# Squares of the gate's rows go between SBUF's quadrants in sixteen SyncE transfers for each half, where they were stored to DRAM and loaded again by ScalarE's queue

## The chip, the cores and the metric

The kernel runs on one core of a Trainium2 chip. The metric is the time of one execution on the device, in microseconds (us), as the median of several runs. Beside the runs there is one profiled execution with its own time; its trace is what the views below are taken from. Engines are called as the profile calls them: PE (TensorE matmul), DVE (VectorE), ACT (ScalarE), POOL (GpSimd), SP (SyncE, which only issues DMA transfers here); SPq and ACTq are the issuing instructions of SP and ACT.

## The reference

One transformer block on a sequence of 2048 rows of 512: softmax attention with 32 heads of 16, then a gated MLP whose gate mixes over the sequence. The change lies in the last stage, so the second half is what has to be seen (`S` = 2048, `D` = 512, `Fh` = 688):

```python
def _B_ref(x, w_in, w_sp, b_sp, w_out):
    z = _gelu(jnp.einsum("bsd,df->bsf", x, w_in))
    z1 = z[..., :Fh]
    z2 = _layernorm(z[..., Fh:], axis=-1)
    g = jnp.einsum("ts,bsf->btf", w_sp, z2) + b_sp[None, :, None]
    return jnp.einsum("bsf,fd->bsd", z1 * g, w_out)

h = x + _A_ref(_layernorm(x, axis=-1), A_wqkv, A_wo)
h2 = h + _B_ref(_layernorm(h, axis=-1), B_w_in, B_w_sp, B_b_sp, B_w_out)
```

## The kernel before

All operands of a matmul are split into a high and a low half-precision part, and a product is made of three matmuls (high by high, high by low, low by high; `mm3`, L108 to L110). Attention and the first projections take the program up to about 1290 us of the span, the making of `z` and of `h` up to about 1455 us, and the last stage, from L1471 on, the rest. Only that last stage is touched.

**The loop.** The gate's 2048 by 2048 product is done by Strassen's scheme in the form that needs seven products for two by two blocks. The loop at L1481 goes over eight pairs of row blocks, `p` = 0 to 7; pair `p` is rows `128 p` and `128 (p + 8)`. In each pass PE runs seven products by name, `b11`, `t1`, `t2`, `b22`, `t3`, `b21`, `n4`, each of 24 matmuls of 128x344 (`product`, L1304). ACT and DVE add the parts (`p1` L1492, `q5` L1496, `v` L1502, the sums at L1509, L1520, L1533, L1543), and POOL multiplies by `z1` (L1510, L1521, L1534). The result is the tile `pr`, 128 rows by two blocks by 688 columns, the gated rows z1 * g.

**The output projection, one pass late.** The gated rows of pair `p` must be turned (rows to columns) before PE can multiply them by `w_out`. They are handled in two halves of the columns: half 1 holds columns 384 to 687, half 0 columns 0 to 383. For each half `level` finds a power of two by which `raise_` (ACT, L1363) scales the rows, and `squares` (L1372) turns them on DVE, which turns 32x32 squares within each group of 32 partitions. What is left is to move whole squares between the four groups of 32 partitions (the quadrants). The tile `squares0` or `squares1` is read by partition group j and square column q, and the tile `whole0` or `whole1` must have at partition group q and place j what stood at partition group j and place q. Each such piece is 32 partitions by 192 numbers of 4 bytes (768 bytes in each partition, 24 KB).

**How it moves before.** `send` (L1385) stores the whole tile (384 KB) to a DRAM scratch `t_scr` with one transfer in ACT's queue; `bring` (L1389) loads it back in four transfers of 96 KB, one for each quadrant of the target, also in ACT's queue, and is called one pass later: `bring(1)` behind `p1`, `bring(0)` behind `q5`. Then `hi` (ACT, L1400) makes the high part of a half, `lo` (DVE, L1409 to L1415) the low part, and `multiply` (L1439) the products with `w_out` on PE. In the pass of pair `p`, `multiply(1, ...)` of pair `p - 1` (16 matmuls of 128x512) stands between the products `b22` and `t3`, and `multiply(0, ...)` (18 matmuls) between `t3` and `b21`. `gather` (DVE, L1454) adds them to the rows of `h`, and `store` (SP, L1457) writes these out.

**What sets the order.** `manual_schedule` (L1471) keeps the program's order on each engine. An engine takes its instructions one after another, so an instruction that waits holds back all that stand behind it on the same engine, DMA issues included. `product` ends with `ask` (L1158), which issues SP's load of a left operand (512 KB) for a product eight places further on; nine such tiles (`op`) exist. `fetch` (L1461) loads the two blocks of `z1` and of `h` for the pair after the current one at the start of each pass. All these are in SP's queue.

**Semaphores of transfers.** Each transfer is counted on one of eight semaphores, taken in turn by the transfers of SP and ACT in program order, and its issue waits until the transfer that last had the same semaphore has landed. So at most eight are on their way.

Of the kernel before, what the change touches and what calls it, by code (L numbers as in the profile page):

```python
# [8 lines left out]
F32 = mybir.dt.float32  # L9
# [10 lines left out]
P = 128  # L20
# [20 lines left out]
HF = 3 * P  # L41
# [18 lines left out]
def block_kernel(ctx: ExitStack, tc: tile.TileContext, x, wqkv, wo, w_in, w_sp4, b_sp, w_out, out):  # L60
# [7 lines left out]
    nc = tc.nc  # L68
# [3 lines left out]
    dram = ctx.enter_context(tc.tile_pool(name="dram", bufs=1, space=DRAM))  # L72
# [15 lines left out]
    h_scr = dram.tile([S, D], F32, name="h_scr")  # L88
    z_scr = dram.tile([S, FH], F32, name="z_scr")
    top_scr = dram.tile([1, 4 * P], F32, name="top_scr")  # L90
    t_scr = [dram.tile([P, 2 * HF], F32, name=f"t{i}_scr") for i in range(4)]
    m_scr = [dram.tile([P, 32], F16, name=f"m{i}_scr") for i in range(2)]
    op_scr = [{n: dram.tile([P, 2, HB, P], F16, name=f"{n}_{p}_scr") for n in TAKEN}
              for p in range(HB)]
# [175 lines left out]
    with ExitStack() as pre:  # L270
# [341 lines left out]
        for g in range(3):  # L612
            a, b = 4 * g, 4 * g + 4
# [54 lines left out]
        for j in range(24):  # L668
            b, n, i = 1 + j // 8, j // 2 % 4, 1 - j % 2
# [117 lines left out]
    with ExitStack() as at:  # L787
# [13 lines left out]
        def product(s, hg, qb, kb, p, t):  # L801

            r = slice(RG * t, RG * t + KM)
            nc.tensor.matmul(s, kst[hg % 2][r, p, kb * P:(kb + 1) * P],  # L804
                             qst[hg * NQ + qb][r, p, :], start=True, stop=True)
# [122 lines left out]
        def send():  # L928
            for i, key in enumerate(measured):
                nc.sync.dma_start(top_scr.rearrange("o (p i) -> (o p) i", i=4)[:, i:i + 1],  # L930
                                  sizes_of[key][:, :1])
# [88 lines left out]
        for key in measured:  # L1020
            for n in (256, 128, 64, 32, 16, 8, 4, 2, 1):
                halve(sizes_of[key], n, 1)
        soon(len(chores) + 4, send)
        soon(len(chores) + 9, spread)
        chores.extend([idle] * 18)
# [18 lines left out]
        for n in range(0, len(units), 2):  # L1044
# [53 lines left out]
            for tok in PAIR if len(later) < 2 else ():  # L1098
                i = int(tok[-1]) if tok[-1].isdigit() else 0
# [16 lines left out]
                elif tok == "H":  # L1116
                    a = 0 if first else 256
# [168 lines left out]
    with ExitStack() as fin:  # L1286
# [3 lines left out]
        f2 = fin.enter_context(tc.tile_pool(name="fin_2", bufs=2))  # L1290
# [5 lines left out]
        def next_g():  # L1296
            banks[0] += 1
            return ps_g[(banks[0] - 1) // 2 % 2].tile([P, 512], F32, name="g")[:, :FC]
# [21 lines left out]
        def weigh_w():  # L1320

            for i in range(2 * 3):
                nc.vector.tensor_reduce(w_top[:, i:i + 1], raw_w[:, i, :], axis=AX.X, op=ALU.max,
                                        apply_absolute_value=True)
# [14 lines left out]
        class Rows:  # L1339
# [43 lines left out]
                    nc.vector.transpose(t.rearrange("p q w i a -> p (w i) q a"), self.pr[:, :, :HF])  # L1383

            def send(self, half):  # L1385
                nc.scalar.dma_start(t_scr[2 * (self.p % 2) + half],
                                  self.turned[half].rearrange("p q w i a -> p (q w i a)"))

            def bring(self, half):  # L1389

                t = self.turned[half] = f2.tile([P, 4, 2, 3, 32], F32, name=f"whole{half}", bufs=1)
                src = t_scr[2 * (self.p % 2) + half].rearrange("(j b) (q c) -> q b j c", j=4, q=4)
                for q in range(4):
                    nc.scalar.dma_start(t[32 * q:32 * q + 32].rearrange("b j w i a -> b j (w i a)"), src[q])

            def hi(self, half):

# [63 lines left out]
        def fetch(p):  # L1461

            got = []
            for name, src, n in (("z1", z_scr, FH), ("h", h_scr, D)):
                for i in range(2):
                    t = fz.tile([P, n], F32, name=f"{name}{i}", bufs=2 + (name == "h"))
                    nc.sync.dma_start(t, src[rows(p, i), :])
                    got.append(t)
            return got

        with tc.manual_schedule(engines={E.PE, E.Activation, E.DVE, E.Pool, E.SP}):  # L1471
            wu = [f1.tile([P, 2 * 3, D], F16, name=f"wu{i}") for i in range(2)]
            raw_w = f1.tile([P, 2 * 3, D], F32, name="raw_w")
            w_top, w_low, w_up, w_down = [f1.tile([P, n], F32, name=f"w_{i}") for i, n in enumerate((6, 1, 1, 1))]
            nc.gpsimd.memset(raw_w[:, 2 * 3 - 1, :], 0.0)
            nc.sync.dma_start(raw_w[:, :5, :], w_out[:5 * P, :].rearrange("(i p) c -> p i c", p=P))
            for r0 in (TW - fn, P - fn):
                nc.sync.dma_start(raw_w[r0:r0 + fn, 5, :], w_out[5 * P:, :])
            nxt = fetch(0)
            now = None  # L1480
            for p in range(HB):  # L1481
                (z1t, z1b, ht, hb), last = nxt, p + 1 == HB
                nxt = None if last else fetch(p + 1)
                before, now = now, Rows(p, (ht, hb))
                bt, bb = bias_up[:, p:p + 1], bias_up[:, p + HB:p + HB + 1]
                A, C, B = [next_g() for _ in range(3)]
                p1, v, q5 = [f0.tile([P, FC], F32, name=n) for n in ("p1", "v", "q5")]
                left, right = now.pr[:, 0, :FC], now.pr[:, 0, FC:FH]
                bl, br = now.pr[:, 1, :FC], now.pr[:, 1, FC:FH]

                product(A, "b11")
                nc.scalar.activation(p1, A, AF.Identity, bias=bt)  # L1492
                if p:
                    before.bring(1)
                product(C, "t1")
                nc.scalar.activation(q5, C, AF.Identity, bias=bb)  # L1496
                if p:
                    before.bring(0)
                else:
                    weigh_w()  # L1500
                product(A, "t2", False)
                nc.scalar.activation(v, A, AF.Identity, bias=bt)  # L1502
                if p:
                    before.hi(1)
                    before.lo(1)
                    before.lower(1, 0, 1)
                    before.lower(0, 0, 1)
                product(C, "b22", False)
                nc.vector.tensor_add(right, C, v)  # L1509
                nc.gpsimd.tensor_mul(right, right, z1t[:, FC:])  # L1510
                if p:
                    accs = [before.multiply(1, w) for w in range(2)]
                    for w in range(2):
                        before.gather(1, w, accs[w])
                    before.hi(0)
                    before.lo(0)
                else:
                    measure_w()
                product(A, "t3", False)
                nc.vector.tensor_add(br, A, q5)  # L1520
                (nc.vector if last else nc.gpsimd).tensor_mul(br, br, z1b[:, FC:])  # L1521
                now.level(1, 0, 1)
                now.raise_(1, 0, 1)
                if p:
                    accs = [before.multiply(0, w) for w in range(2)]
                    for w in range(2):
                        before.gather(0, w, accs[w])
                        before.store(w)
                if not last:
                    now.squares(1)  # L1530
                    now.send(1)
                product(B, "b21")
                nc.vector.tensor_add(left, B, p1)  # L1533
                (nc.vector if last else nc.gpsimd).tensor_mul(left, left, z1t[:, :FC])  # L1534
                if last:
                    now.level(0, 0)
                    for w in range(2):
                        now.turn(1, w)
                        now.split(1, w)
                    now.lower(1, 0, 1)  # L1540
                    now.raise_(0, 0)
                product(A, "n4", False)
                nc.vector.scalar_tensor_tensor(bl, A, bb, z1b[:, :FC], op0=ALU.add, op1=ALU.mult)  # L1543
                if last:
                    now.level(0, 1)
                    now.raise_(0, 1)
                else:
                    now.level(0, 0, 1)
                    now.raise_(0, 0, 1)
                    now.squares(0)  # L1550
                    now.send(0)
            accs = [now.multiply(1, 0)]
            now.turn(0, 0)
            now.split(0, 0)
            accs.append(now.multiply(1, 1))
            now.turn(0, 1)
            now.gather(1, 0, accs[0])
            now.split(0, 1)
            now.gather(1, 1, accs[1])
            now.lower(0, 0, 1)  # L1560
            acc = now.multiply(0, 0)
            now.gather(0, 0, acc)
            now.store(0)
            acc = now.multiply(0, 1)
            for c in (slice(0, D // 2), slice(D // 2, D)):
                now.gather(0, 1, acc, c)
                now.store(1, c)
# [29 lines left out]
```

## Time and profile before

| | |
|---|---|
| Median of 3 runs | 1727.85 us (1726.92 to 1728.79) |
| The profiled execution | 1733.43 us, of which the span of the trace is 1731.7 us |
| Mean granted TensorE clock in it | 0.997 |
| PE busy from 0 to 1420 us | 1410.34 us |
| PE busy from 1420 to 1732 us | 295.05 us of 312.00 |
| DVE, ACT, POOL busy from 1420 to 1732 us | 135.38, 66.73, 51.70 us |
| DMA share and rate from 1420 to 1732 us | 0.57, 181 GB/s |

How to read the views that follow. A row of waits has the waiting engine and line, what it waited for, the total, the number of times and the longest. A row of the timeline has start, duration, engine, line, operation, output <- inputs, and in brackets the idle time of the engine just before it and what ended that. A row of windows has the stretch, its length, the busy time of PE, PEld, DVE, ACT and POOL with their instruction counts, the granted TensorE clock as a share of full speed, the busy share of the DMA engines, and their GB/s. A row for a line has the number of instructions after the x and least, median and greatest duration in ns.

### The profile page before, as it was taken

To read this page: it belongs to the slowest core of one execution; us is meant where nothing else is said; L and a number is where in the kernel's file an instruction comes from. 1 tells how busy PE (TensorE), PEld (TensorE's weight loads), DVE (VectorE), ACT (ScalarE), POOL (GpSimd) and SP (SyncE) were. 2 spreads that over 40 slices of the span, in tenths; PEclk is the share of its full clock that TensorE was granted. 3 is DMA by queue.
4 is the path that set the end of the run, shared out by engine and by line. 5 is a ranking of instruction groups with operands and counts; after the bars stand their busy time and mean duration, and the time that the engine had idled before them with its cause. 6 is when DMAs were issued, how large, how long until landed. Compare 5 with 4: busy or idle time off the path is not lost.

```text
span 1731.7 us, 36651 instructions
## 1 busy us (share of the span) xinstructions
PE 1705.4 (98%) x13499; PEld 644.6 (37%) x13499; DVE 1449.7 (84%) x3051; ACT 1318.0 (76%) x2584; POOL 812.9 (47%) x1062
## 2 busy tenths in 40 slices
PE   9999999999999999999999999999999999999999
PEld 4433222222222222222222222222226666565555
DVE  7688999999999999999999999999927886432434
ACT  4334999999999999999999999999984554111111
POOL 1332867775772268686677857300004676100100
PEclk9999999999999999999999999999999999999999
DMA  5534332342231235355245343310124455676661
GB/s 182 162 97 146 98 88 82 95 102 68 75 71 30 62 100 135 99 151 149 80 142 144 120 124 106 75 23 9 45 64 136 142 180 198 217 229 204 181 196 53
DMA packets 194013, 201.53 MB, mean 116 GB/s; under 512 B 66824, under 2 KB 142920, under 8 KB 193832
## 3 DMA queue, kind: packets, MB, share of 16 engines
q1 hardware_dynamic: 181448, 182.53, 36.4%
q10 hardware_dynamic: 12384, 16.65, 2.9%
q8 instruction: 106, 1.74, 0.4%
q14 instruction: 75, 0.61, 0.1%
HBM read 127.61 MB, written 71.44 MB: 115 GB/s over the span
## 4 chain that ended last, share of the span: by engine, by line
PE 71%; DVE 15%; DMA 6%; POOL 2%; issue 2%; ACT 2%; SPq 1%; ACTq 1%; DVEq 0%; POOLq 0%
PE pv L829 25%; PE s L804 17%; PE m L224 9%; DVE mx L229 7%; PE acc L108 4%; PE acc L110 4%; PE acc L109 4%; DMA whole<-t_scr 2%; PE g L110 2%; PE g L108 2%; PE g L109 2%; DVE ab L238 1%; DVE og L839 1%; DMA rc<-r_scr 1%; DVE rs_t L125 1%
## 5 line engine op out<-in xcount | busy, mean ns | idle before, releaser
L813 ACT ACTIVATE pt<-s 128x512 f32<-128x512 f32 x1968 | 1006.2, 637 | 5.5 <-PE m L224 4.4
L229 DVE TENSOR_REDUCE mx<-m 128x1 f32<-128x512 f32 x1510 | 947.5, 682 | 12.7 <-PE m L224 3.9
L804 PE MATMUL s<-qst,kst 50*128 50x512 f16 x2048 | 604.3, 379 | 0.2
L829 PE MATMUL pv<-pt,vst 128*32 128x256 f32 (+1 forms) x6056 | 598.1, 466 | 4.1 <-DVE og L839 1.3
L224 PE MATMUL m<-kst,qst 48*128 48x512 f16 x1510 | 452.5, 381 | 0.0
L804 PEld LDWEIGHTS <-kst 50*128 50x128 f16 x2048 | 132.0, 94 | 352.0 <-issue 322.9
L829 PEld LDWEIGHTS pv<-pt,vst 128*32 128x32 f32 x6056 | 119.5, 108 | 290.7 <-issue 277.3
L224 PEld LDWEIGHTS <-qst 48*128 48x128 f16 x2048 | 159.2, 93 | 173.7 <-issue 124.3
L224 PE MATMUL m<-uvs,qst 48*128 48x512 f16 x504 | 190.5, 380 | 0.6 <-DVE mx L229 0.6
L246 POOL TENSOR_SCALAR nm<-nm 128x16 f32<-128x16 f32 x32 | 6.6, 206 | 361.2 <-DVE nm L243 361.2
L238 DVE CUSTOM_DVE_ANT_0 ab<-m,ab 128x512 f32<-128x512 f32 x252 | 170.5, 677 | 2.7 <-ACT ab L234 2.7
L234 ACT ACTIVATE ab<-m 128x512 f32<-128x512 f32 x252 | 157.3, 624 | 16.5 <-PE m L224 15.8
L1363 ACT ACTIVATE pr<-pr,up 128x304 f32<-128x304 f32 (+1 forms) x32 | 17.0, 574 | 118.8 <-DVE up L1317 118.8
L990 POOL TENSOR_TENSOR op<-raw,op 128x512 f16<-128x512 f32 x80 | 92.9, 1161 | 6.0
L913 POOL TENSOR_TENSOR raw<-raw 128x512 f32<-128x512 f32 (+1 forms) x84 | 83.3, 991 | 6.7
L918 POOL TENSOR_TENSOR acc_sp<-acc_sp,raw 128x512 f32<-128x512 f32 x63 | 80.4, 1276 | 4.5
L108 PE MATMUL acc<-wi,hT 128*128 128x344 f16 x256 | 79.1, 309 | 1.4 <-ACT hT L99 1.4
L110 PE MATMUL acc<-wi,hT 128*128 128x344 f16 x256 | 79.1, 309 | 0.3 <-DVE hT L105 0.3
L109 PE MATMUL acc<-wi,hT 128*128 128x344 f16 x256 | 79.1, 309 | 0.0
L1510 POOL TENSOR_TENSOR pr<-pr,z 128x344 f32<-128x344 f32 x8 | 7.3, 914 | 137.8 <-DVE pr L1509 111.6
L1413 DVE TENSOR_TENSOR pT<-whole,pT 128x256 f16<-128x256 f32 x14 | 5.3, 422 | 73.7 <-ACT pT L1400 73.7
L910 POOL TENSOR_SCALAR raw<-raw 128x512 f32<-128x512 f32 (+1 forms) x88 | 52.3, 594 | 19.8 <-DMA raw<-in_wqkv 12.4
(247 smaller groups left out, 2293.4 us busy)
## 6 DMA issues: line engine op xcount, KB each, us to landing
raw<-in_w_sp SPq DMA_DIRECT2D x128, 256.0 KB
s_scr<-op SPq DMA_DIRECT2D x64, 256.0 KB
op<-s_scr SPq DMA_DIRECT2D x32, 512.0 KB
a_scr<-op SPq DMA_DIRECT2D x48, 256.0 KB
op<-a_scr SPq DMA_DIRECT2D x24, 512.0 KB
o_scr<-og SPq DMA_DIRECT2D x64, 128.0 KB
qst<-q_scr SPq DMA_DIRECT2D x192, 32.0 KB
kst<-k_scr SPq DMA_DIRECT2D x48, 128.0 KB
```

The source lines that it names most:

```text
L108: nc.tensor.matmul(ps, lh, rh, start=first, stop=False, **kw)
L109: nc.tensor.matmul(ps, lh, rl, start=False, stop=False, **kw)
L110: nc.tensor.matmul(ps, ll, rh, start=False, stop=last, **kw)
L224: nc.tensor.matmul(acc, q[r, p, c], keys[r, p], start=True, stop=True)
L229: nc.vector.reduce_max(at(t, e if t else e - 1), acc, axis=AX.X)
L234: nc.scalar.activation(ab[0], acc, AF.Abs)
L238: nc.vector.tensor_tensor_reduce(ab[0], acc, ab[0], 0.5, LOW, ALU.add, ALU.max, at(0, 0))
L804: nc.tensor.matmul(s, kst[hg % 2][r, p, kb * P:(kb + 1) * P], qst[hg * NQ + qb][r, p, :], start=True, stop=True)
L813: nc.scalar.activation(pts[p, kb][:, t, :], s, AF.Exp, scale=scales_[hg // 2])
L829: nc.tensor.matmul(pv[0][32 * j:32 * j + 32, a:b], vst[hg % 2][:, c:c + 32], pts[j % 2, kb][:, j // 2, a:b], start=kb == 0, stop=kb == NB - 1,
L913: pool.tensor_mul(got[0] if n else acc, got[0], got[0])
L990: chores.append((lambda: pool.tensor_sub(t[0][:, 1], of(), t[0][:, 0]), TT))
```

## The change

The store to DRAM and the load back are gone, with the scratch `t_scr` and the method `bring`. `send` now makes the target tile `whole` at once and issues sixteen transfers from SBUF to SBUF, one for each pair of quadrants, in SP's queue. `send` keeps its places: behind `squares(1)` in the middle of the pass and behind `squares(0)` at its end. The line numbers of the changed kernel are one lower from L92 on, and four lower behind `bring`, eight lower behind the loop's calls of it.

```diff
-    t_scr = [dram.tile([P, 2 * HF], F32, name=f"t{i}_scr") for i in range(4)]
...
             def send(self, half):
-                nc.scalar.dma_start(t_scr[2 * (self.p % 2) + half],
-                                  self.turned[half].rearrange("p q w i a -> p (q w i a)"))
-
-            def bring(self, half):
-
-                t = self.turned[half] = f2.tile([P, 4, 2, 3, 32], F32, name=f"whole{half}", bufs=1)
-                src = t_scr[2 * (self.p % 2) + half].rearrange("(j b) (q c) -> q b j c", j=4, q=4)
-                for q in range(4):
-                    nc.scalar.dma_start(t[32 * q:32 * q + 32].rearrange("b j w i a -> b j (w i a)"), src[q])
+
+                t, w = self.turned[half], f2.tile([P, 4, 2, 3, 32], F32, name=f"whole{half}", bufs=1)
+                for j in range(4):
+                    for q in range(4):
+                        nc.sync.dma_start(w[32 * q:32 * q + 32, j], t[32 * j:32 * j + 32, q])
+                self.turned[half] = w
...
                 nc.scalar.activation(p1, A, AF.Identity, bias=bt)
-                if p:
-                    before.bring(1)
                 product(C, "t1")
                 nc.scalar.activation(q5, C, AF.Identity, bias=bb)
-                if p:
-                    before.bring(0)
-                else:
+                if not p:
                     weigh_w()
```

SP's queue over one pass of the loop in the kernel before, from the last load of a left operand ahead of the stores to the end of the next `fetch`, with the waits left out:

```order
L1162 DMA op<-a_2_scr 128x2048
L1457 DMA out_y<-h_23086 128x512
L1457 DMA out_y<-h_23088 128x512
L1162 DMA op<-a_2_scr 128x2048
L1162 DMA op<-a_3_scr 128x2048
L1467 DMA z_23648<-z_scr 128x688
L1467 DMA z_23650<-z_scr 128x688
L1467 DMA h_23652<-h_scr 128x512
L1467 DMA h_23654<-h_scr 128x512
```

The same place in the changed kernel:

```order
L1161 DMA op<-a_2_scr 128x2048
L1453 DMA out_y<-h_23082 128x512
L1453 DMA out_y<-h_23084 128x512
L1389 DMA whole_23599<-squares_23594 32x192 x16
L1161 DMA op<-a_2_scr 128x2048
L1161 DMA op<-a_3_scr 128x2048
L1389 DMA whole_23681<-squares_23679 32x192 x16
L1463 DMA z_23698<-z_scr 128x688
L1463 DMA z_23700<-z_scr 128x688
L1463 DMA h_23702<-h_scr 128x512
L1463 DMA h_23704<-h_scr 128x512
```

Sixteen transfers of half 1 now stand behind the two stores and ahead of two loads of left operands, and sixteen of half 0 ahead of the four of `fetch`.

ACT's queue over one pass in the kernel before (`t_scr<-squares` is `send`, `whole<-t_scr` is `bring`, `pT<-whole` is `hi`, first of half 1, then of half 0):

```order
L1363 ACTIVATE pr<-pr,up_23545 128x304 x2
L1386 DMA t_scr<-squares_23576 128x768
L1363 ACTIVATE pr<-pr,up_23638 128x384 x2
L1386 DMA t_scr<-squares_23645 128x768
L1492 ACTIVATE p_23660<-g,fig_1847 128x344
L1394 DMA whole_23690<-t_scr 32x4x192 x4
L1496 ACTIVATE q_23662<-g,fig_1847 128x344
L1394 DMA whole_23722<-t_scr 32x4x192 x4
L1502 ACTIVATE v<-g,fig_1847 128x344
L1400 ACTIVATE pT_23754<-whole_23690 128x768
L1400 ACTIVATE pT_23812<-whole_23722 128x768
```

And in the changed kernel:

```order
L1362 ACTIVATE pr<-pr,up_23563 128x304 x2
L1362 ACTIVATE pr<-pr,up_23672 128x384 x2
L1488 ACTIVATE p_23710<-g,fig_1843 128x344
L1490 ACTIVATE q_23712<-g,fig_1843 128x344
L1494 ACTIVATE v<-g,fig_1843 128x344
L1396 ACTIVATE pT_23794<-whole_23599 128x768
L1396 ACTIVATE pT_23852<-whole_23681 128x768
```

ACT's seven activations of these rows keep their order among each other, and no transfer is left in this queue. The orders of PE, DVE and POOL are the same in both kernels.

With the waits shown, the stores of one pass and the first eight of the sixteen transfers of half 1 in the changed kernel (DMAHW0 to DMAHW7 are the eight semaphores of transfers):

```order
L1453 DMA out_y<-h_23082 128x512 [waits DMAHW5_49,DVE_49]
L1453 DMA out_y<-h_23084 128x512 [waits DMAHW6_49,DVE_49]
L1389 DMA whole_23599<-squares_23594 32x192 [waits DMAHW7_49,DVE_49,Activation_49]
L1389 DMA whole_23599<-squares_23594 32x192 [waits DMAHW0_49]
L1389 DMA whole_23599<-squares_23594 32x192 [waits DMAHW1_49,DVE_49]
L1389 DMA whole_23599<-squares_23594 32x192 [waits DMAHW2_49]
L1389 DMA whole_23599<-squares_23594 32x192 [waits DMAHW3_49]
L1389 DMA whole_23599<-squares_23594 32x192 [waits DMAHW4_49]
L1389 DMA whole_23599<-squares_23594 32x192 [waits DMAHW5_49]
L1389 DMA whole_23599<-squares_23594 32x192 [waits DMAHW6_49]
```

The seventh of them waits for the semaphore that the first store has, and the ninth to the sixteenth wait for the first to the eighth.

## The prediction

> **What bounds the kernel now.** The page comes first: PE is busy nearly all of the span, so a change pays only if it takes idle time or slow time from PE.
>
> ```profile
> span 1731.7 us, 36651 instructions
> PE 1705.4 (98%) x13499; PEld 644.6 (37%) x13499; DVE 1449.7 (84%) x3051; ACT 1318.0 (76%) x2584; POOL 812.9 (47%) x1062
> ```
>
> Next the waits of the last stage (1480 to 1732 us), where the change lies. PE has one kind of wait there, for `hi` of ACT, and ACT in turn waits for the loads of `whole`:
>
> ```profile
> ACT v L1502 <- DMA whole<-t_scr: 26.6, 6, 5.8
> ACT pT L1400 <- DMA whole<-t_scr: 25.1, 10, 4.6
> PE acc L108 <- ACT pT L1400: 10.8, 6, 3.8
> ```
>
> PE's timeline shows the six one by one. All stand before the first matmul of `multiply(1, 0)`, in passes 1 to 6; none stands before half 0.
>
> ```profile
> 1496.64 0.39 PE L108 MATMUL acc<-wu,pT 128*128 128x512 f16 x1 [3.19 <-ACT pT L1400]
> 1530.57 0.39 PE L108 MATMUL acc<-wu,pT 128*128 128x512 f16 x1 [0.21 <-ACT pT L1400]
> 1566.37 0.61 PE L108 MATMUL acc<-wu,pT 128*128 128x512 f16 x1 [3.76 <-ACT pT L1400]
> 1602.17 0.39 PE L108 MATMUL acc<-wu,pT 128*128 128x512 f16 x1 [0.83 <-ACT pT L1400]
> 1635.08 0.39 PE L108 MATMUL acc<-wu,pT 128*128 128x512 f16 x1 [0.86 <-ACT pT L1400]
> 1669.11 0.39 PE L108 MATMUL acc<-wu,pT 128*128 128x512 f16 x1 [2.00 <-ACT pT L1400]
> ```
>
> The windows right behind the two longest waits and behind the one of 2.00 us show a second cost, in the column after POOL's, the granted clock:
>
> ```profile
> 1496.60:1501.00 4.40, 4.36 (x13) 1.59 (x14) 2.93 (x9) 0.32 (x1) 0.91 (x1) 0.61 0.60 160
> 1566.40:1572.60 6.20, 6.20 (x16) 2.19 (x17) 2.88 (x9) 0.84 (x1) 0.91 (x1) 0.52 0.41 125
> 1669.00:1672.00 3.00, 2.89 (x14) 1.24 (x15) 2.84 (x9) 0.21 (x2) 0.45 (x1) 1.00 0.90 209
> ```
>
> After 3.19 and 3.76 us of idleness PE ran at 0.61 and 0.52 of its clock for some microseconds; after 2.00 us at full clock.
>
> **What it removes.** The load back starts late: `bring(1)` stands in ACT's queue behind half 0's store and `p1`, although half 1 was ready long before. One pass, on DVE, ACT and in the chain of waits:
>
> ```profile
> 1510.76 0.46 DVE L1380 STREAM_TRANSPOSE squares<-pr 128x128 f32<-128x128 f32 x2
> 1519.90 0.98 DVE L1383 STREAM_TRANSPOSE squares<-pr 128x768 f32<-128x768 f32 x1 [1.25 <-ACT pr L1363]
> 1521.45 2.24 ACTq L1394 DMA_DIRECT2D whole<-t_scr  x4
> 1523.19 6.41 DMA whole<-t_scr
> 1528.53 0.55 ACT L1502 ACTIVATE v<-g,fig 128x344 f32<-128x344 f32 x1 [4.25 <-DMA whole<-t_scr]
> 1529.67 0.84 ACT L1400 ACTIVATE pT<-whole 128x768 f16<-128x768 f32 x1 [0.59 <-DMA whole<-t_scr]
> ```
>
> Half 1 was turned at 1511.22, its load issued from 1521.45 and landed at 1529.60. Without the wait PE would start these matmuls at 1530.57 - 0.21 = 1530.36. In the changed kernel the move of half 1 can start at 1511.3. `hi(1)` has to start by 1530.36 - 0.84 - 0.05 = 1529.5, and nothing of ACT stands before it but `v`, which no transfer holds up any more. That leaves 18 us for the move.
>
> If the move keeps its dates in all passes, this goes: the waits, 3.19 + 0.21 + 3.76 + 0.83 + 0.86 + 2.00 = 10.85 us; and the slow clock behind two of them, 4.40 x (1 - 0.61) = 1.72 and 6.20 x (1 - 0.52) = 2.98, together 4.70 us. Sum 15.55 us. ACT's queue also loses ten issues a pass; ACT is no bound here, and I count them at nothing.
>
> The Trainium skill, "TensorE: Matmul & The Clock Gate", Part 1, says that the array falls to half clock after an idle window of about 3.4 us and needs about 3.4 us of work to come back. The trace agrees in kind, though the fall came at 3.19 us already. By that page each fall costs about 1.7 us, an estimate, and the sum would be 14.25 us.
>
> **What it adds.** Thirty-two issues a pass in SP's queue. The trace has no transfer of this shape; the nearest rows:
>
> ```profile
> L1386 ACTq DMA_DIRECT2D t_scr<-squares x14: 326/344/345, 1480.1 to 1691.7; - x14
> L1394 ACTq DMA_DIRECT2D whole<-t_scr x56: 309/444/1792, 1485.7 to 1695.8; - x56
> L152 SPq DMA_DIRECT2D kst<-ones x4: 664/684/783, 137.5 to 163.8; - x4
> 273.93 3.78 SPq L195 DMA_DIRECT2D qst<-q_scr  x6
> SPq L264 <- DMA m_scr<-mturned: 30.2, 28, 2.3
> ```
>
> For one issue the low bound is the store of the same tile, 0.34 us and a gap of 0.05, so 0.39. Six loads of 32 KB take 3.78 us, 0.63 each. The high bound is the only transfer from SBUF to SBUF in the trace, 0.684 and the gap, 0.73. The old load, of the same pieces of 768 bytes, took 2.24 / 4 = 0.56 in the pass above. I take 0.39 to 0.56: the new form is two plain strides on both sides, as the store's was. For the landing the low bound is the small store at L261: 30.2 / 28 = 1.08 us behind an issue like the store's 0.34, so 1.4; the high bound is the 6.41 above, in a busy DMA.
>
> **Does half 0 keep its date?** It is turned at 1520.88, and PE comes to its first matmul here:
>
> ```profile
> 1534.27 0.75 DVE L1454 SCALAR_TENSOR_TENSOR h<-acc,low,h 128x512 f32<-128x512 f32 x1 [0.83 <-PE acc L1449]
> 1537.56 0.38 PE L108 MATMUL acc<-wu,pT 128*128 128x512 f16 x1
> ```
>
> Without the wait that is 1537.35. The low part is used two matmuls (0.43) later; `hi(0)` and `lo(0)` take 0.84 + 0.95 and gaps of 0.1, so `whole0` must have landed by 1535.9. On SP the order is: sixteen of half 1 from 1511.22, two loads of left operands (0.74), sixteen of half 0. With c for one issue and L for the landing, half 0 is late when 32 c + L + 0.74 exceeds 24.7 us. With L = 1.4 that is c over 0.70. At c = 0.73 the lateness is 0.8 us a pass, at c = 0.39 with L = 6.41 there are 5 us to spare. With at most eight on their way, a landing of 6.41 also holds the ninth back: 6.41 + 7 x 0.39 + 6.41 = 15.6 us after 1520.88, 0.6 us late. So bad ends cost up to 1 us a pass, 7 us in all. A long landing is unlikely: the large loads that made DMA busy there stand behind the sixteen in the same queue, only two of them before.
>
> **What is queued behind the new waits on SP.** SP's rows of that pass before:
>
> ```profile
> 1509.14 1.38 SPq L1457 DMA_DIRECT2D out_y<-h  x2
> 1510.61 2.61 SPq L1162 DMA_DIRECT2D op<-a_scr  x2
> 1514.44 2.89 SPq L1467 DMA_DIRECT2D z<-z_scr  x2
> 1517.42 0.86 SPq L1467 DMA_DIRECT2D h<-h_scr  x2
> 1518.33 8.89 SPq L1162 DMA_DIRECT2D op<-s_scr  x4
> 1530.39 0.32 SPq L1162 DMA_DIRECT2D op<-a_scr  x1
> 1541.38 1.38 SPq L1457 DMA_DIRECT2D out_y<-h  x2
> ```
>
> The sixteen of half 1 wait for DVE's turning at 1511.22, and behind them wait the two operand loads, which go from 1510.6 to about 1518. The sixteen of half 0 wait until 1520.88; behind them the loads of `z1` and `h` go from 1514.4 to about 1528, and the next operand loads from 1518.3 to about 1530. An operand is asked for eight products ahead, over 30 us, and `z1` is used a pass later; so 12 us are covered. If that cover were gone, PE would wait for an operand in every pass. SP has the room. Its 13 other issues a pass are like these:
>
> ```profile
> L1162 SPq DMA_DIRECT2D op<-s_scr x32: 319/320/1252, 1395.0 to 1664.1; - x32
> L1467 SPq DMA_DIRECT2D h<-h_scr x16: 372/423/1381, 1458.8 to 1654.6; - x16
> ```
>
> At 0.32 to 0.42 and the gap they are about 5.4 us, the new ones 12.5 (c = 0.39), 17.9 (0.56) or 23.4 (0.73), against a period of about 32 us (the stores above are 32.24 apart). Behind the load at 1530.39 SP idled until the stores at 1541.38; the delay goes into that idleness, and the stores keep their date. Pass 0 is no exception: its half 1 went out at 1480.10, and PE asked for it 13 us later, at 1496.64 - 3.19 = 1493.45.
>
> ```profile
> 1480.10 0.33 ACTq L1386 DMA_DIRECT2D t_scr<-squares  x1
> ```
>
> **The sum.** 1733.43 - 15.55 = 1717.9 us for the profiled execution. The median of the runs is 1727.85, 5.6 us less. The pass at 1566 fits that difference: its wait and slow clock cost 3.76 + 2.98 = 6.74, against a middle of 0.86 for the other five waits, 5.9 more. If the common run lacks that accident, it can gain 15.55 - 5.9 = 9.7, and ends at 1718.2, the same place. If instead recording costs 5.6 us evenly, it ends at 1712.3. I take 1718.
>
> **The rivals.**
>
> *Something of the stall stays* (up to 7 us, above): 1718 to 1725. For it: the DMA share is 0.60 to 0.90 in the windows; against it: large loads now come after the moves.
>
> *It is hidden anyway*, within 0.2% of 1727.85 (about what a measurement can tell from no change), 1724.4 to 1731.3. For it: in a usual pass the wait is below 1 us. Against it: the waits of 3.19 and 2.00 and one fall of the clock are no accident of one pass. It takes a new wait of 1 to 2 us in each pass; price 1727.
>
> *SP becomes the bound* (slower). Place: half 0's sixteen, at the end of 32 issues. It decides where the seven passes lose what was gained: 15.55 / 7 = 2.2 us late a pass, c = 0.70 + 2.2 / 32 = 0.77. The slowest group of four loads in ACT's queue took 3.41 us, 0.85 each; with that c half 0 is 32 x 0.85 + 1.4 + 0.74 - 24.7 = 4.6 us late, over 3.19, so the clock falls too, by the mean of 2.35: 7 x (4.6 + 2.35) = 48.7, less 15.55, gives 1766.6. That row:
>
> ```profile
> 1553.64 3.41 ACTq L1394 DMA_DIRECT2D whole<-t_scr  x4
> ```
>
> For it: four times the issues; against it: only a jammed DMA gave 0.85, the other shapes stay below 0.70.
>
> *The small transfers run one after another.* Each waits for the landing of the one before, 1.4 us: 32 x 1.4 + 5.4 = 50.2 us of SP against 32, 18 us a pass, 7 x 18 - 15.55 = +110, 1844. Against it: the six loads in 3.78 us are 0.63 each, below one landing, so they overlap. The Trainium skill, "DMA: Bandwidth & Descriptors", Rules for kernel authors, speaks for it: many small transfers should be made one large, since below 64 KB one pays mostly overhead; its section on the anatomy of one DMA gives about 2.0 us fixed for each, by which, unlapped, the loss would be 7 x (64 + 5.4 - 32) = 262 us, an estimate. The trace's six loads disagree.
>
> **How the numbers follow.** Forecast (the waits go, 1711 to 1720) 0.62; part of the stall stays 0.18; hidden 0.07; SP the bound 0.11; one after another 0.02. The range holds the first two: from 1711, just below the 1712.3, to 1725. Faster: 0.62 and nearly all of 0.18, 0.79; within 0.2%: 0.08; slower 0.13.
>
> **What would show it.** Right: no wait of PE for `hi` in passes 1 to 6 and a granted clock of 1.00 there; `hi(1)` starting right behind `v`; SP's sixteen in 6 to 9 us; passes about 32.1 us apart. Wrong: PE waiting before half 0's first matmul, issues over 0.70 us, a wait of PE for an operand, or a later fall of the clock at a new place.

## The result: no change, and the profile after

| | Median | Least to greatest | Runs |
|---|---|---|---|
| Before | 1728.67 us | 1725.23 to 1733.07 | 20 |
| Changed kernel | 1728.32 us | 1725.31 to 1730.83 | 20 |

The ratio is 0.9999 with a 95% interval of 0.9992 to 1.0006. The forecast was 1718 us and a chance of 0.79 for faster. The profiled execution of the changed kernel took 1728.91 us. In its page PE is as busy as before, and ACT's queue (q10) has kept 2304 of its 12384 packets, since the rest now goes by SP's (q1):

```profile
span 1727.1 us, 36869 instructions
PE 1703.1 (99%) x13499; PEld 644.2 (37%) x13499; DVE 1450.7 (84%) x3051; ACT 1317.5 (76%) x2584; POOL 812.9 (47%) x1062
q1 hardware_dynamic: 192200, 188.04, 36.9%
q10 hardware_dynamic: 2304, 5.64, 0.8%
```

PE's waits in the last stage, from its timeline (the idle time just before each instruction stands in the bracket):

```profile
1494.05 0.39 PE L107 MATMUL acc<-wu,pT 128*128 128x512 f16 x1 [0.31 <-ACT pT L1396]
1505.43 0.39 PE L107 MATMUL acc<-wu,pT 128*128 128x512 f16 x1 [4.22 <-ACT pT L1396]
1506.42 0.61 PE L109 MATMUL acc<-wu,pT 128*128 128x512 f16 x1 [0.26 <-DVE pT L1405]
1603.63 0.39 PE L109 MATMUL acc<-wu,pT 128*128 128x512 f16 x1 [0.17 <-DVE pT L1405]
1637.63 0.39 PE L107 MATMUL acc<-wu,pT 128*128 128x512 f16 x1 [2.42 <-ACT pT L1396]
1638.62 0.39 PE L109 MATMUL acc<-wu,pT 128*128 128x512 f16 x1 [0.39 <-DVE pT L1405]
```

Only the first, of 0.31 us, is for half 1. The others are for half 0, which PE never waited for before. Behind the two long ones the granted clock (the column after POOL's) falls again:

```profile
1505.40:1511.00 5.60, 5.32 (x17) 1.94 (x18) 3.43 (x7) 0.99 (x2) 0.91 (x1) 0.70 1.01 358
1637.60:1642.00 4.40, 3.98 (x11) 1.39 (x12) 3.07 (x7) 0.50 (x2) 0.91 (x1) 0.65 1.03 365
```

The waits add up to 7.77 us, the slow clock to 5.60 x 0.30 + 4.40 x 0.35 = 3.22 us, 10.99 together. 1728.91 - 10.99 = 1717.9 us, the same floor that the prediction worked out from the trace of before. So the old waits went, and new ones of the same size came. Nothing ties the two to each other; that the time stayed the same is a coincidence.

Where half 0 lost its time is in SP's timeline. These are rows from the moves of pass 0 and of pass 1; the dots stand for the other loads and the stores between them:

```profile
1480.33 11.54 SPq L1389 DMA_DIRECT2D whole<-squares  x16
1491.98 0.99 SPq L1161 DMA_DIRECT2D op<-a_scr  x2
1493.06 10.01 SPq L1389 DMA_DIRECT2D whole<-squares  x16
1503.17 1.00 SPq L1463 DMA_DIRECT2D z<-z_scr  x2
...
1513.12 10.96 SPq L1389 DMA_DIRECT2D whole<-squares  x16
1524.18 1.00 SPq L1161 DMA_DIRECT2D op<-a_scr  x2
1525.28 10.78 SPq L1389 DMA_DIRECT2D whole<-squares  x16
```

The row for the line, and the end of the chain of waits in pass 1:

```profile
L1389 SPq DMA_DIRECT2D whole<-squares x224: 507/588/1917, 1480.3 to 1699.4; - x112
...
1501.85 0.59 SPq L1389
1502.48 1.82 DMA whole<-squares
1504.48 0.04 issue
1504.53 0.85 ACT pT L1396
```

One issue takes 0.588 us and a gap of 0.046, so 0.634; where no issue has another wait, sixteen take 16 x 0.634 = 10.1 us. In pass 0 half 0 was turned at 1485.6, but SP was busy with half 1 until 1491.9, and half 0 landed at 1504.3. PE had been ready at 1501.2.

The wait of 2.42 us in pass 5 has another beginning, also in the chain of waits:

```profile
1607.10 8.84 DMA out_y<-h
1615.96 0.51 SPq L1389
1616.51 0.59 SPq L1389
...
1623.19 5.34 DMA op<-a_scr
1628.54 0.51 SPq L1389
```

The seventh transfer of half 1 shares its semaphore with the store of an output block, and that store took 8.84 us to land, behind the 3.7 MB of loads that SP had issued in one go from 1600.4 on, when half 0's transfers were through. A transfer of half 0 then stood in the same way for an operand load.

### The profile page after: what moved, and what is told of

The parts are those of the page before. It is cut to its first block, busy times and chain, and to the rows that moved or that the text cites. A ratio compares the mean times of both kernels' runs of the same rounds, so it can differ in the third digit from the quotient of the medians.

```text
span 1727.1 us, 36869 instructions
## 1 busy us (share of the span) xinstructions
PE 1703.1 (99%) x13499; PEld 644.2 (37%) x13499; DVE 1450.7 (84%) x3051; ACT 1317.5 (76%) x2584; POOL 812.9 (47%) x1062
## 3 DMA queue, kind: packets, MB, share of 16 engines
q10 hardware_dynamic: 2304, 5.64, 0.8%
q8 instruction: 106, 1.74, 0.4%
## 4 chain that ended last, share of the span: by engine, by line
PE 70%; DVE 15%; DMA 4%; POOL 3%; SPq 3%; issue 2%; ACT 2%; ACTq 0%; DVEq 0%; POOLq 0%
PE pv L828 25%; PE s L803 17%; PE m L223 9%; DVE mx L228 7%; PE acc L107 3%; PE acc L109 3%; PE acc L108 3%; PE g L107 2%; PE g L109 2%; PE g L108 2%; SPq L1389 2%; DVE ab L237 1%; DVE og L838 1%; DVE rs_t L124 1%; DMA out_y<-h 1%
## 5 line engine op out<-in xcount | busy, mean ns | idle before, releaser
L894 POOL TENSOR_SCALAR raw<-raw,figs 128x512 f32<-128x512 f32 (+1 forms) x84 | 55.8, 670 | 8.6 <-DMA raw<-in_wo 7.9
```

## The experiments

Two theories were set against each other. A: SP's issues are the cost, 32 in a row at 0.63 us, which the short pass 0 has no room for. B: the small transfers, or a busy DMA, land late wherever they are issued. Each ratio is to the kernel before in the same session.

**Half 1 alone by the new way.**

```diff
             def send(self, half):
+                if half:
+                    (sixteen transfers in SP's queue, as in the changed kernel)
+                    return
                 nc.scalar.dma_start(t_scr[...], ...)
...
-                if p:
-                    before.bring(1)
```

> Half 1 goes by the sixteen transfers in SP's queue, half 0 by DRAM in ACT's queue as before. Theory A (SP's issues are the cost: 32 in a row at 0.63 us bring half 0 late, above all in the short pass 0; the move of half 1 alone has room): no wait of PE for half 1, waits for half 0 below 1 us in all, granted clock 1.00 in all passes, 1717 to 1720 us. Theory B (small transfers or the busy DMA land late wherever they are issued, so that the loss only changes its place): waits of 4 us and more and a fall of the clock remain, 1725 to 1729 us.

Measured: 1726.95 us, ratio 0.9986 (0.9976 to 0.9996). PE waited for half 1 in passes 1 to 6, 8.2 us in all. That is B's number, but neither theory's reason. ACT's timeline of pass 4:

```profile
1583.84 0.34 ACTq L1393 DMA_DIRECT2D t_scr<-squares  x1
1584.23 0.55 ACT L1499 ACTIVATE p<-g,fig 128x344 f32<-128x344 f32 x1 [1.44 <-DVE squares L1383]
1586.34 0.55 ACT L1501 ACTIVATE q<-g,fig 128x344 f32<-128x344 f32 x1 [1.56 <-PE g L110]
1587.12 7.18 ACTq L1401 DMA_DIRECT2D whole<-t_scr  x4
1594.35 0.55 ACT L1507 ACTIVATE v<-g,fig 128x344 f32<-128x344 f32 x1 [7.47 <-DMA whole<-t_scr]
1594.80 0.83 ACT L1407 ACTIVATE pT<-whole 128x768 f16<-128x768 f32 x1
```

Half 1 had long landed, but `hi(1)` stands behind `v`, and `v` behind the four load issues of half 0, which took from 1587.12 to 1594.30. Each of them waits for the transfer that last had its semaphore: the second was issued at 1588.39, when an operand load had landed, and the fourth at 1593.99, when a load of `z1` had. So half 0's load in ACT's queue is enough to make PE wait, with half 1 there in time.

**Half 0 alone by the new way.**

```diff
             def send(self, half):
+                if not half:
+                    (sixteen transfers in SP's queue)
+                    return
                 nc.scalar.dma_start(t_scr[...], ...)
...
-                if p:
-                    before.bring(0)
-                else:
+                if not p:
                     weigh_w()
```

> Half 0 goes by the sixteen transfers in SP's queue, half 1 by DRAM in ACT's queue as before (its load is no longer behind half 0's store there, so issued 1 to 2 us earlier). Theory A: half 0 is never late, since its sixteen start at once when it is turned (16 x 0.63 + 1.8 = 12 us, 15 allowed); waits for half 1 remain at 1 to 3 us in pass 1 and below 1 us elsewhere; 1720 to 1726 us. Theory B: half 0 late as in the changed kernel, 3 to 5 us in pass 1, and half 1 too; 1728 us or more.

Measured: 1717.54 us, ratio 0.9933 (0.9920 to 0.9946), better than A had it: PE has no wait in the last stage. Half 0's sixteen start when it is turned, and with half 0 out of ACT's queue the load of half 1, whose store landed long before, holds up only `q5`, for a time that PE does not feel.

**Half 1's transfers shared by two queues.**

```diff
-                        nc.sync.dma_start(w[32 * q:32 * q + 32, j], t[32 * j:32 * j + 32, q])
+                        e = nc.scalar if half and q % 2 else nc.sync
+                        e.dma_start(w[32 * q:32 * q + 32, j], t[32 * j:32 * j + 32, q])
```

> The changed kernel, with eight of half 1's sixteen transfers issued by ACT (idle there) and eight by SP; bytes, pieces and route are the same. Theory A: half 1 takes 5 us instead of 10 of SP, half 0 starts when it is turned and lands 4 to 5 us earlier; no wait of PE in passes 2 to 7, at most 0.5 us in pass 1, clock 1.00; 1717 to 1720 us. Theory B: half 0 lands as late as in the changed kernel, waits of 4 us and more in pass 1; 1726 to 1729 us.

Measured: 1719.59 us, ratio 0.9945 (0.9931 to 0.9958), as A had it, with the same bytes and pieces. One wait of PE is left, of 1.8 us in pass 1: ACT's eight issues hold up `p1` there, and the product `t2` adds to the bank that `p1` reads.

```profile
1488.12 0.31 PE L107 MATMUL g<-t,op 128*128 128x344 f16 x1 [1.82 <-ACT p L1489]
```

**The load of half 1 from DRAM issued earlier, nothing else changed in the kernel before.**

```diff
                     now.send(1)
+                    if p:
+                        now.bring(1)
...
                     now.raise_(0, 0, 1)
+                    if not p:
+                        now.bring(1)
...
-                if p:
-                    before.bring(1)
```

> The kernel before with one thing moved: the load of half 1 from DRAM is issued in ACT's queue right behind its store (in pass 0 behind raise_ of half 0) instead of in the next pass behind p1, some 8 us earlier. If the date of the load, and not the route by DRAM, made PE wait before, its waits go from about 10 us to below 2 us and the time to 1717 to 1721 us, as fast as the best form of the move within SBUF. If the route is what costs (store and load each land late in a busy DMA), waits of 5 us and more remain: 1725 us or more.

Measured: 1727.08 us, ratio 0.9986 (0.9976 to 0.9996), a miss. PE waits 5.5 us for half 1 and 3.1 us for `p1`. In pass 1 `p1` stands behind the early load and half 0's store, and that store was held until 1489.1 for the semaphore of a load of `h`:

```profile
1489.56 0.55 ACT L1492 ACTIVATE p<-g,fig 128x344 f32<-128x344 f32 x1 [4.68 <-DMA h<-h_scr]
```

The time is that of the other branch, but not for its reason, as the way by DRAM in SP's queue shows below. An earlier load of half 1 does not free `v` from half 0's. With half 1 alone by the new way this says the same twice: an earlier date of half 1 alone is not enough.

**A second profiled execution of both kernels, unchanged.**

> The kernel before, unchanged, for a second look. If the wait of 3.76 us with its fall of the clock in pass 3 was an accident of the one profiled execution, the waits of PE for hi of half 1 come to 5 to 8 us here, with the long one in pass 1, and ACT's v is held behind the load of half 0 in every pass. If it is the rule, 10 us and more again.

> The changed kernel, unchanged, for a second look. Theory A (32 issues at 0.63 us; pass 0 is too short for them): the wait of about 4 us for half 0 with its fall of the clock stands in pass 1 again, and each transfer is issued 0.63 us behind the last. The wait of 2.4 us in pass 5, where the seventh transfer stood for a slow store, is an accident and falls in another pass or in none. Theory B (transfers land late): the waits move about freely and pass 1 is not marked out.

Measured: before 1729.21 us in one run, its waits in passes 1 and 4 the long ones:

```profile
1497.42 0.39 PE L108 MATMUL acc<-wu,pT 128*128 128x512 f16 x1 [3.47 <-ACT pT L1400]
1597.92 0.61 PE L108 MATMUL acc<-wu,pT 128*128 128x512 f16 x1 [2.51 <-ACT pT L1400]
```

They are 7.9 us in all, and the 3.76 of pass 3 is not there. The changed kernel took 1728.85 us in one run, and its long wait stands in pass 1 again:

```profile
1505.14 0.61 PE L107 MATMUL acc<-wu,pT 128*128 128x512 f16 x1 [4.67 <-ACT pT L1396]
```

Its other waits are 0.39 to 0.94 us, for half 0 in the later passes. So pass 1 has a long wait in both executions of each kernel, and the size of the later waits changes from one execution to the next.

**Four of the sixteen pieces copied by POOL.** The pieces with j = q stay in their quadrant.

```diff
-                        nc.sync.dma_start(w[32 * q:32 * q + 32, j], t[32 * j:32 * j + 32, q])
+                        e = nc.gpsimd.tensor_copy if j == q else nc.sync.dma_start
+                        e(w[32 * q:32 * q + 32, j], t[32 * j:32 * j + 32, q])
```

> The changed kernel, with the four pieces of each half that stay in their quadrant copied by POOL; SP issues twelve transfers a half instead of sixteen. Theory A (the number of issues in SP's row is the cost): half 0 of pass 0 lands 5 us earlier, the wait of 4.2 us in pass 1 falls to at most 0.5 us with its fall of the clock, 1717 to 1721 us. Theory B (landing in a busy DMA): the wait in pass 1 stays over 3 us, 1726 to 1729 us.

Measured: 1716.77 us, ratio 0.9935 (0.9921 to 0.9949). PE has no wait left. From 1480 to 1700 us of this kernel, of the changed one and of the one before, PE's busy time (the first number after the comma) is:

```profile
1480.00:1700.00 220.00, 220.00 (x1398) 136.70 (x1396) 87.66 (x203) 37.92 (x65) 37.69 (x78) 1.00 0.49 173
```

```profile
1480.00:1700.00 220.00, 212.23 (x1323) 129.44 (x1321) 81.71 (x192) 35.31 (x60) 18.26 (x20) 0.98 0.52 176
```

```profile
1480.00:1700.00 220.00, 209.15 (x1299) 127.08 (x1297) 78.22 (x185) 36.73 (x61) 17.38 (x19) 0.98 0.65 197
```

Eight issues fewer a pass, each of them 0.63 us, are enough: SP finished half 0 of pass 0 at 1496.9 instead of 1503.1. This form also moves a quarter less by DMA; the one with two queues moved all of it.

**The way by DRAM, but in SP's queue.**

```diff
             def send(self, half):
-                nc.scalar.dma_start(t_scr[...], ...)
+                nc.sync.dma_start(t_scr[...], ...)
+                self.bring(half)
...
-                    nc.scalar.dma_start(t[32 * q:32 * q + 32]..., src[q])
+                    nc.sync.dma_start(t[32 * q:32 * q + 32]..., src[q])
```

with the later calls of `bring` left out.

> Both halves go through DRAM as before, but store and load are issued one behind the other in SP's queue at the places of the changed kernel's sixteen: five issues instead of sixteen, and one more landing to wait for. Theory A (issues on SP and whom they hold are the cost, not the route): about 2 us of issues and 2 to 5 us of the store's landing, so 5 to 7 us a half instead of 10 to 11; ACT's v is held by nothing; 1717 to 1721 us. If the route by DRAM is slow in itself, half 0 comes as late as in the changed kernel: 1725 us or more.

Measured: 1717.88 us, ratio 0.9939 (0.9926 to 0.9953), no wait of PE. In a later pass a half is through SP in about 4 us:

```profile
1516.27 0.32 SPq L1386 DMA_DIRECT2D t_scr<-squares  x1
1518.72 1.74 SPq L1395 DMA_DIRECT2D whole<-t_scr  x4
```

The store and its landing take 2.45 us, the four loads 1.74. So the route by DRAM by itself is not the cost.

**Only pass 0 mended.** Half 1 of pass 0 goes by DRAM in ACT's queue; the other halves as in the changed kernel.

```diff
             def send(self, half):
+                if self.p or not half:
+                    (sixteen transfers in SP's queue)
+                    return
                 nc.scalar.dma_start(t_scr[...], ...)
...
-                if p:
+                if p == 1:
                     before.bring(1)
```

> The changed kernel, but half 1 of pass 0 alone goes by DRAM in ACT's queue as before; the other thirteen halves go by the sixteen transfers. Theory A: half 0 of pass 0 starts when it is turned and lands in time, so the wait of 4.2 to 4.7 us in pass 1 and its fall of the clock (1.7 to 3 us) go, about 6 to 7 us, and the waits of 0.4 to 2.4 us in the passes after stay: 1720 to 1723 us. If pass 1 is not marked out and the loss only moves to a later pass, 1726 us or more.

Measured: 1722.13 us, ratio 0.9971 (0.9959 to 0.9983). The wait in pass 1 is gone; 3.5 us of waits for half 0 are left in two later passes. So pass 0 is worth 1728.32 - 1722.13 = 6.2 us by the medians, which come from two sessions, and (0.9999 - 0.9971) x 1728 = 4.8 us by the two ratios. The waits and slow clock of pass 1 in the profile are 4.22 + 0.26 + 0.31 + 1.68 = 6.5.

**Each piece in two transfers.**

```diff
-                        nc.sync.dma_start(w[32 * q:32 * q + 32, j], t[32 * j:32 * j + 32, q])
+                        for i in range(2):
+                            nc.sync.dma_start(w[32 * q:32 * q + 32, j, i], t[32 * j:32 * j + 32, q, i])
```

> The changed kernel, with each piece moved in two transfers of half the width: 64 issues a pass of 12 KB each, the same bytes. If an issue costs 0.63 us whatever its size, SP needs 64 x 0.63 + 5.4 = 45.7 us a pass against the 32 of PE, and the program becomes SP's: 7 x 14 = 96 us more than the 1718 without waits, and up to 20 us for falls of the clock: 1800 to 1840 us. If an issue costs by its bytes, 10 us a half stay and the time is near 1728 us.

Measured: 1872.59 us, ratio 1.0838 (1.0817 to 1.0859). The issue costs the same for half the bytes:

```profile
L1390 SPq DMA_DIRECT2D whole<-squares x448: 507/588/1555, 1480.0 to 1842.4; - x150
```

The time is worse than expected, since I had counted SP's issues alone. Half 1's thirty-two cannot start before half 0 has landed and been multiplied, added and stored: the passes are 52 to 57 us apart instead of 45.7, and the granted clock is 0.82 from 1480 to 1850 us.

**Sixteen loads from DRAM instead of four.** As the way by DRAM in SP's queue, with each load split into its pieces.

```diff
-                for q in range(4):
-                    nc.sync.dma_start(t[32 * q:32 * q + 32]..., src[q])
+                for j in range(4):
+                    for q in range(4):
+                        nc.sync.dma_start(t[32 * q:32 * q + 32, j]..., src[j, q])
```

> As dram_sync, but each load of four pieces is split into its four pieces of 32 partitions by 192 numbers: one store and sixteen loads a half in SP's queue, the same shape as the changed kernel's transfers with DRAM as the source. If the shape or the number is what an issue costs, 0.58 us and more each, half 0 comes later than in the changed kernel by the store's landing: waits of 3 us and more in most passes, 1735 to 1770 us. If the cost of 0.59 belongs to a transfer from SBUF to SBUF, an issue takes 0.32 to 0.44 us here, the sixteen about 6 to 7 us, and the time is 1718 to 1722 us.

Measured: 1762.81 us, ratio 1.0203 (1.0182 to 1.0224), with 32.2 us of waits for `hi` and falls of the clock behind them.

```profile
L1396 SPq DMA_DIRECT2D whole<-t_scr x224: 303/419/1556, 1486.3 to 1733.7; - x112
```

An issue takes 0.42 us here, as in the second of the two cases that I had named, but the time came out in the range of the first: I had not counted the landing of the store in the second. The same shape is dearer from SBUF (0.59) than from DRAM, and one piece from DRAM costs as much as four did (0.44). It is the number of issues that costs, and here the store's landing, 4 to 7 us before them.

## Why the prediction was wrong

**What was right.** The floor. 1733.43 - 15.55 = 1717.9 was the sum, and the three forms that leave PE no wait took 1716.8, 1717.5 and 1717.9 us. The wait for half 1 and its fall of the clock went, but for 0.31 us in pass 1, and `hi(1)` starts right behind `v` from pass 2 on. The pass at 1566 was an accident of the profiled execution, as the prediction supposed: in the second execution it did not come back, though pass 4 had a wait of 2.51 us and a fall in its stead, and 1733.43 lies above all twenty runs of before.

**The step that failed** is the sentence "Pass 0 is no exception". It checked half 1 there, and not half 0. The condition for half 0 (32 c + L + 0.74 against 24.7 us, with c for one issue and L for the landing) was worked out for a later pass. By the prediction's own trace PE, without its wait, would come to half 0 of pass 0 at about 1500.4, and `whole0` would have to land by about 1498.9, 18.8 us after half 1 was turned at 1480.1. These are 5.9 us less. From the start of `b21` to that place PE needs 28.1 us in either pass, but half 1 was turned 7.8 us after `b21` began in pass 0 (1472.26) and 2.0 us after in pass 1 (1509.20). Of the difference 3.9 us are the 18 matmuls of `multiply(0)`, which stand ahead of `b21` in pass 1 and which pass 0 does not have. The rest is mostly DVE's: in pass 0 it made the low part of `w_out` (`wu`) until 1474.98 and only then began on the rows, 2.5 us after PE had done `t3`; in pass 1 it began at once.

```profile
1470.92 4.06 DVE L1335 SCALAR_TENSOR_TENSOR wu<-raw_w,w,wu 128x512 f16<-128x512 f32 x6 [0.67 <-ACT wu L1334]
1474.90 0.51 DVE L1520 TENSOR_TENSOR pr<-g,q 128x344 f32<-128x344 f32 x1
```

At the measured c = 0.634 and L = 1.82 the left side is 22.8 us: on time in a later pass, 4.0 us late in pass 0, where the wait was 4.22. At c = 0.39 nothing would have shown; at 0.56, the other end of what was taken, 1 us and more would have.

**A size that was off.** c was taken as 0.39 to 0.56, after the store of the same tile and the load of the same pieces. It was 0.634, the number that six loads of 32 KB gave, and above both of the rows that were preferred. The bounds 0.39 to 0.73 held it. The landing of 1.82 lay near the low end, as argued.

**"Large loads come after the moves"** was right and was taken for harmless. The loads go out in one row just ahead of the next stores, and a store that lands late behind them holds the seventh transfer of half 1 by their common semaphore. The order of SP's rows showed both. This and the thin margin of half 0 are what is left between 1722.13 and the floor, some 4 to 5 us. In the profiled execution of the kernel with only pass 0 mended it is four waits of 0.39 to 1.59 us and no fall of the clock. In pass 3 of it the two sixteens took 12.08 and 10.29 us and the last piece landed after 3.73, longer than c and L above would give. How the 4 to 5 us divide between the two causes was not measured.

**Why PE waited before** was only half told. The prediction named the late load of half 1. Moving that load alone gave 1727.08, and removing it 1726.95. But two things held `hi(1)`, half 1's own load and, through `v`, half 0's load, which waited in ACT's queue for half 0's store to land, and they ended close together. In pass 3, with the longest wait, it was half 0: its store took 9.75 us to land, its load went behind that, and `hi(1)` starts right behind `v`. In pass 1 `v` was let go at 1495.09 and half 1 landed last, by some 0.2 us. In the four others (waits of 0.21 to 2.00 us, no fall) `hi(1)` waited 0.59 to 1.70 us more for half 1. These are rows of passes 1, 3 and 6; those without an engine are from the chain of waits:

```profile
1487.87 7.84 DMA whole<-t_scr
1495.09 0.55 ACT L1502 ACTIVATE v<-g,fig 128x344 f32<-128x344 f32 x1 [5.79 <-DMA whole<-t_scr]
1495.74 0.84 ACT L1400 ACTIVATE pT<-whole 128x768 f16<-128x768 f32 x1
1553.15 9.75 DMA t_scr<-squares
1565.04 0.55 ACT L1502 ACTIVATE v<-g,fig 128x344 f32<-128x344 f32 x1 [7.39 <-issue]
1565.49 0.83 ACT L1400 ACTIVATE pT<-whole 128x768 f16<-128x768 f32 x1
1668.22 0.84 ACT L1400 ACTIVATE pT<-whole 128x768 f16<-128x768 f32 x1 [1.70 <-DMA whole<-t_scr]
```

So with half 1 early the other hold was left. Taking half 0 out of ACT's queue ended both (1717.54 us). The row of waits told of it: `v` waited 26.6 us for `whole`, though `v` needs nothing of it.

**The rivals.** "Something of the stall stays" was the right kind, priced at 7 us at most where it was 10.4. "It is hidden anyway" has the measured time, at a chance of 0.07, by a new wait as it said, though of one pass above all. "SP becomes the bound" had the right place and needed c over 0.77; doubling the issues showed that cliff. "One after another" fell: the landing is 1.82 us and the issues 0.634 apart.

## What to carry to other kernels

A date that a transfer has to keep must be checked in every pass in which the cover differs, above all the first and the last, where some of the hiding work is missing. Count small transfers by the issuing queue's time, the number of instructions times 0.3 to 0.6 us here, and not by bytes; and look at what stands behind a held instruction on an engine that does not need the data at all. The cheapest cures here were to have five issues instead of sixteen in the same queue (1717.9 us), or to give only the half that has the late date to the new way (1717.5 us), or to let a little-used engine copy the pieces that need no transfer (1716.8 us).

## What the runs showed of the hardware that was not expected

The TensorE clock fell after shorter idle times than the first trace showed. After waits of 2.42, 2.51 and 2.07 us it was 0.65, 0.64 and 0.70 in the window behind (the changed kernel, the second execution of before, and the kernel with the early load). After 2.00 us in the first trace and 1.85 us with half 1 alone moved it stayed at 1.00, and so it did after 2.59 us in the kernel with sixteen loads from DRAM, so that the length of the wait alone does not decide. This is the window behind the 2.07 us:

```profile
1532.50:1536.00 3.50, 3.42 (x11) 1.27 (x12) 2.94 (x9) 0.60 (x2) 0.92 (x1) 0.70 0.42 152
```

The Trainium skill, "TensorE: Matmul & The Clock Gate", Part 1, puts the idle window at about 3.4 us; the measurement decides: here a wait of a little over 2 us could already cost a fall, and need not. An issue of a transfer from SBUF to SBUF took 0.588 us with pieces of 768 and of 384 bytes alike, one of the same shape from DRAM 0.419 us, and the store of the whole tile 0.32 us.
